# Polysketch attention and an ELU block: pairs of query groups, and the first w_out products earlier

## The chip, the cores and the metric

The kernel runs on one core of one Trainium2 chip. The metric is the time of one execution in device microseconds (us); the median of three runs is given. A separate profiled execution shows where the time lies; its span (first to last instruction) is a few microseconds shorter than the time.

The engines by the names of the profile: PE is TensorE (matrix products; PEld is its loading of weights), DVE is VectorE, ACT is ScalarE, POOL is GpSimd, SP issues transfers.

## The reference

Attention by a sketched polynomial kernel, without a mask, and then a two-layer block with ELU:

```python
q, k, v: (4, 4, 1088, 32)      # batch, heads, sequence, head_dim
S1, S2:  (8, 32)
w_in:    (128, 2048)           # w_out: (2048, 128)

def phi(x):                                    # 64 features per token and head
    a = einsum('rd,bhsd->bhsr', S1, x)
    b = einsum('rd,bhsd->bhsr', S2, x)
    return einsum('bhsi,bhsj->bhsij', a, b).reshape(..., 64)

q_p, k_p = phi(q), phi(k)
kv  = einsum('bhsf,bhsd->bhfd', k_p, v)
z   = sum(k_p, axis=2)
num = einsum('bhsf,bhfd->bhsd', q_p, kv)
den = einsum('bhsf,bhf->bhs', q_p, z)[..., None] + 1e-6
x   = num / den                                # to (4352 tokens, 128)
h   = x @ w_in
g   = where(h > 0, h, exp(min(h, 0)) - 1)
out = g @ w_out
```

The inputs come as 8-byte floats. The kernel reads them as pairs of 32-bit words; for the weights it builds a rounded 4-byte float on the chip in five steps (`round_a` to `round_e`, of which `round_b` is on ScalarE and the others on VectorE).

## The kernel before

The 4352 tokens are 68 half tiles of 64 tokens. Eight half tiles make a query group of 512 tokens; there are nine groups, the last with 256. w_in and w_out are cut into eight blocks `cp` (two times 128 columns or rows each). A step is one block of one group: two products with w_in (`mm1`, tile `h`), ELU on ScalarE and VectorE (`elu_a`, `elu_d`, tiles `e` and `gg`), two products with w_out (`mm2`, tile `o`), which follow two steps later. Groups 0 and 1 share their way through the blocks, since the blocks are still being rounded; later groups run one after the other:

```python
steps = [(0, 0), (0, 1), (1, 0), (1, 1)] + [(g, cp) for cp in range(2, NP) for g in range(2)]
steps += [(g, cp) for g in range(2, NQ) for cp in range(NP)]
```

The attention of the groups from 2 on is put between the steps. A query site holds the products of two groups: `q5` multiplies the features of a group by kv (two halves f), `q1` projects the q of the next group:

```python
def queries(g5, g1, n):
    hs[steps[n]] = [psum.tile([P, 512], F32, name="h", tag="h", bufs=4) for c in range(2)]
    ps = hs[steps[n]] + [psum.tile([P, 512], F32, name="qps", tag="aux") for _ in range(2)]
    if g5 is not None: q5(g5, ps, 0)
    if g1 is not None: q1(g1, ps, g5 is None)
    if g5 is not None: q5(g5, ps, 1)

def q1(g, ps, start=True):
    for c in range(4):                       # a quarter of the group's tokens
        for h in range(H):
            r = slice(D * h, D * h + D)
            for b, t, k, m in parts(g, c):   # two parts where a quarter crosses a batch boundary
                nc.tensor.matmul(ps[h][32 * c:32 * c + 32, P + 64 * k:P + 64 * (k + m)],
                                 SWq[r, b]..., qT[b][r, t:t + m, :]..., tile_position=(D * h, 32 * c))
...
    at(13, queries, None, 2, 14)
    mid(13, q1_out, 2)
    for g in range(2, NQ):
        n = NP * (g - 1)
        n2, n4, n5 = (13, 14, 15) if g == 2 else (n + 3, n + 4, n + 6)
        late(n2, q2, g)                      # denominator and outer product, VectorE
        (mid if g == 2 else late)(n4, q4, g) # transpose of the features, VectorE
        at(n5, queries, g, None if last else g + 1, n5 + 1)
        mid(n5, q5_out, g)                   # x of the group, ScalarE
        if not last: mid(n5, q1_out, g + 1)  # transposes, VectorE
```

`at(n, ...)`, `mid(n, ...)` and `late(n, ...)` put an operation behind the `mm1` of step n, between its two ELU halves, or behind them. `RA(i)`, `RB(i)` are the first two rounding steps of item i of the list `order`, `RC(i)` the last three (four VectorE operations):

```python
order = [(0, 1, 0), (1, 1, 0), (0, 0, 1), (1, 0, 1), (2, 1, 0), (2, 0, 1)] + [(cp, 1, 1) for cp in range(3, NP)]
# (block, w_in?, w_out?)
```

The opening computes the keys of batch 0, the x of groups 0 and 1 and their first products one after another. Its end:

```python
    q5_early(0)              # x of group 0: products xps, copies xg
    q1_second()              # q of group 1, into a tile of the pool "aux"
    mm1_first()              # group 0, block 0
    ...
    RC(1)
    elu_a(0, 0, 0); elu_a(0, 0, 1)
    mm1(0, 1)
    q2(1, 2)                 # group 1: denominator and outer product (qp)
    q4_early(1)              # transposes on TensorE (qtp), copies (qpT)
    for c in range(2): elu_d(0, 0, c)
    round_w(round_c, 2)
    RA(3); RB(3)
    round_w(round_d, 2)
    q5_early(1)              # x of group 1
    keep_warm(1)             # one product that nobody needs (idle)
    round_w(round_e, 2)
    round_w(round_c, 3)
    for c in range(2):
        elu_a(0, 1, c); elu_d(0, 1, c)
        round_w(round_e if c else round_d, 3)
    KC(0)
```

After it the loop begins at step 2 with `mm1(1, 0)` and then `mm2(0, 0)`.

Of the kernel before, what the change touches and what calls it, by code (L numbers as in the profile page):

```python
# [27 lines left out]
def kernel(  # L28
# [8 lines left out]
    moe_w_out: bass.AP,  # L37
    out: bass.AP,
):

# [6 lines left out]
    nc = tc.nc  # L49
# [276 lines left out]
        feats[b, half] = kp  # L326


    def KO_first(t0, t1):
        if t0 == 0:  # L330
            feats[0, 0] = work.tile([P, 5, H, R, R], F32, name="kp", tag="kp", bufs=3)
        a_ = kf_ps[0][:, 64 * t0:64 * t1].rearrange("p (m x r) -> p m x r", x=2, r=R)[:, :, 1, :]
        b_ = feats[0][:, 0, t0:t1].rearrange("p t h r -> p (t h) r")
        m = (t1 - t0) * H
        nc.vector.tensor_mul(feats[0, 0][:, t0:t1].rearrange("p t h i j -> p (t h) i j"),
                             _ap(a_, list(a_.ap[1:]) + [[0, R]]), _ap(b_, [[R, m], [0, R], [1, R]]))

    def KO_pool():
        kp = feats[0, 1] = work.tile([P, 5, H, R, R], F32, name="kp", tag="kp", bufs=3)
        ab = feats[0][:, :, 5:].rearrange("p x t h r -> p (t h) x r")  # L340
        outer(kp[:, :KT - 5].rearrange("p t h i j -> p (t h) i j"), ab, nc.gpsimd)

# [72 lines left out]
    NH = B * NT  # L417
    NQ = (NH + 7) // 8
    qn = [min(8, NH - 8 * g) // 2 for g in range(NQ)]
    abw, ans, qp, qpT, xg = {}, {}, {}, {}, {}  # L420
    pws = [const.tile([P, H * 4, R + 1], F32, name=f"pw{i}") for i in range(2)]
    for pw in pws:
        nc.gpsimd.memset(pw[:, :, R:], 1e-6)

# [32 lines left out]
        return p[:, :128].rearrange("p (t h r) -> p h t r", t=4, h=H)  # L457

    def q1_second():
        p = psum.tile([P, 512], F32, name="abwp", tag="aux")  # L460
        for i in range(4):
            for u in range(2):
                b, t = half_tile(1, 2 * i + u)
                nc.tensor.matmul(p[64 * u:64 * u + 64, i * 96:i * 96 + 96], qT[b][:, t, :],  # L464
                                 SW[:].rearrange("p h x r -> p (h x r)"), skip_group_check=True,
                                 tile_position=(0, 64 * u))
        abw[1] = work.tile([P, H * 4, 3 * R], F32, name="abw1", tag="abq1", bufs=1)
        nc.scalar.copy(abw[1][:].rearrange("p (h t) y -> p h t y", h=H),
                       p[:, :384].rearrange("p (t h y) -> p h t y", t=4, h=H))

    def parts(g, c):

        n = qn[g] // 2
        k = 0
        while k < n:
            b, t = half_tile(g, n * c + k)
            m = min(n - k, NT - t)
            yield b, t, k, m
            k += m
# [3 lines left out]
    def q1(g, ps, start=True):  # L483
        for c in range(4):
            for h in range(H):
                r = slice(D * h, D * h + D)
                for b, t, k, m in parts(g, c):
                    nc.tensor.matmul(ps[h][32 * c:32 * c + 32, P + 64 * k:P + 64 * (k + m)],  # L488
                                     SWq[r, b].rearrange("p x r -> p (x r)"),
                                     qT[b][r, t:t + m, :].rearrange("p t s -> p (t s)"), start=start, stop=True,  # L490
                                     skip_group_check=True, tile_position=(D * h, 32 * c))
        abw[g] = ps

    def q1_out(g):
        ps, n = abw[g], qn[g]
        abw[g] = work.tile([P, H * 4, 4 * R], F32, name="abw", tag="abw", bufs=2)
        for h in range(H):
            nc.vector.transpose(abw[g][:, n * h:n * h + n, :].rearrange("p m y -> p (m y)"), ps[h][:, P:P + 32 * n])  # L498

    def q2(g, parts=1):  # L500
        q2_den(g)
        q2_out(g, parts)

    def q2_den(g, zq=None):
        m = H * qn[g]
        x = abw[g][:, :m, :]
        pw = pws[g % 2]
        if zq is None:
            nc.vector.tensor_mul(pw[:, :m, :R], x[:, :, R:2 * R], x[:, :, 2 * R:3 * R])
        else:  # L510
            nc.vector.tensor_mul(pw[:, :m, :R].rearrange("p (h t) r -> p h t r", h=H),
                                 x[:, :, R:2 * R].rearrange("p (h t) r -> p h t r", h=H), zq)
        den = work.tile([P, 4 * H], F32, name="den", tag="den")
        nc.vector.tensor_reduce(den[:, :m], pw[:, :m], axis=AX, op=ADD)
        nc.vector.reciprocal(den[:, :m], den[:, :m])
        an = work.tile([P, 4 * H, R], F32, name="an", tag="an")
        nc.vector.tensor_mul(an[:, :m], x[:, :, R:2 * R], _ap(den[:, :m], [[1, m], [0, R]]))
        ans[g] = an

# [23 lines left out]
    def q5_early(g):  # L543
        xp = [psum.tile([P, 512], F32, name="xps", tag="aux") for _ in range(2)]
        for h in range(H):
            for w in range(2):
                nc.tensor.matmul(xp[w][D * h:D * h + D, :256], kvS[64 * w:64 * w + 64, h, :],  # L547
                                 qpT[g][64 * w:64 * w + 64, h].rearrange("p m s -> p (m s)"),
                                 skip_group_check=True, tile_position=(64 * w, D * h))
        xg[g] = work.tile([P, 512], F32, name="xg", tag="xg", bufs=2)  # L550
        to = xg[g][:].rearrange("p (m w s) -> p w m s", w=2, s=P)
        for w, copy in enumerate((nc.scalar.copy, nc.vector.tensor_copy if g else nc.scalar.copy)):
            copy(to[:, w], xp[w][:, :256].rearrange("p (m s) -> p m s", s=P))

    def q4(g):

        m = H * qn[g]
        qpT[g] = work.tile([P, 4 * H, 2, 32], F32, name="qpT", tag="qpT", bufs=2)
        nc.vector.transpose(qpT[g][:, :m].rearrange("p m f s -> p (m f s)"),  # L559
                            qp[g][:, :m].rearrange("p m i j -> p (m i j)"))  # L560

    def q5(g, ps, f):
        n = qn[g]
        for h in range(H):
            for c in range(4):
                r = slice(32 * c, 32 * c + 32)
                for j, (b, t, k, m) in enumerate(parts(g, c)):
                    nc.tensor.matmul(ps[c][D * h:D * h + D, 64 * k:64 * (k + m)], kvq[r, b, f, h, :],  # L568
                                     qpT[g][r, n * h + 2 * k:n * h + 2 * (k + m), f, :],
                                     start=(f == 0 and j == 0), stop=(f == 1),  # L570
                                     skip_group_check=True, tile_position=(32 * c, D * h))
        xg[g] = ps

    def q5_out(g):
        ps, n = xg[g], 32 * qn[g]
        xg[g] = work.tile([P, 512], F32, name="xg", tag="xg", bufs=2)
        for c in range(4):

            o = n * c if g < NQ - 1 else n * (2 * (c % 2) + c // 2)
            nc.scalar.copy(xg[g][:, o:o + n], ps[c][:, :n])  # L580

    def queries(g5, g1, n):

# [94 lines left out]
    KF(0)  # L678
    transp(qT, "q", 0, 0, 8)
    q1_first()  # L680
    KO_first(0, 5)
    KO_pool()
    Z_first()
    zq = q1z_first()
    RA(0)
# [19 lines left out]
    mm1(0, 1)  # L705
    q2(1, 2)
    q4_early(1)
    for c in range(2):
        elu_d(0, 0, c)
    round_w(round_c, 2)  # L710
    RA(3)
    RB(3)
    round_w(round_d, 2)
    q5_early(1)
    keep_warm(1)
    round_w(round_e, 2)
    round_w(round_c, 3)
    for c in range(2):
        elu_a(0, 1, c)
        elu_d(0, 1, c)  # L720
        round_w(round_e if c else round_d, 3)
    KC(0)

# [12 lines left out]
    def late(n, f, *a):  # L738
        extra.setdefault((n, 1), []).append((f, *a))

    for n, i in ((2, 3), (3, 4), (4, 6), (5, 5), (6, 7), (8, 8), (10, 9), (12, 10)):
        if i > 3:
            at(n - 1, RA, i)
            late(n - 1, RB, i)
        if i > 3:
            at(n, RC, i, i == 7)

    late(2, make_Sxp)
    late(2, make_SWq)
    late(3, Z_share, 0)  # L750
    late(8, KV_first)
    zls = {}

# [12 lines left out]


    for b, (n_t, n_f, n_o, n_a, n_z) in enumerate(
            ((4, 6, (7, 9), 11, 12), (15, 16, (17, 18), 19, 20), (18, 19, (24, 27), 30, 32)), 1):
        at(n_t, transp, kT, "k", b, 0, NT)  # L770
        at(n_f, KF_late, b)
        late(n_f, KF_late_out, b)
# [3 lines left out]
        late(n_a, sums_out, b)  # L776
        at(n_z, turn, b)
        late(n_z, turned, b)
    late(7, transp, qT, "q", 1, 0, NT)
    at(21, transp, qT, "q", 2, 0, NT)  # L780
    at(30, transp, qT, "q", 3, 0, NT)
    at(13, queries, None, 2, 14)
    mid(13, q1_out, 2)
    for g in range(2, NQ):
        n = NP * (g - 1)
        n2, n4, n5 = (13, 14, 15) if g == 2 else (n + 3, n + 4, n + 6)
        late(n2, q2, g)
        (mid if g == 2 else late)(n4, q4, g)
        last = g + 1 == NQ
        at(n5, queries, g, None if last else g + 1, n5 + 1)  # L790
        mid(n5, q5_out, g)
        if not last:
            mid(n5, q1_out, g + 1)

    N = len(steps)
    for n in range(2, N + 2):
# [12 lines left out]
        g, cp = steps[n - 2]  # L809
        if g == NQ - 1:  # L810
            mm2_last(cp, cp == 0, cp == NP - 1)
        else:
            mm2(g, cp, cp == 0, cp == NP - 1)
            if cp == NP - 1:
                fin1(g)
# [30 lines left out]
```

## Time and profile before

| | |
|---|---|
| time, median of 3 | 281.13 us (281.09 to 281.94) |
| span of the profiled execution | 277.7 us |
| granted TensorE clock | 1.000 |
| PE busy | 271.4 us |
| DVE busy | 180.0 us |
| ACT busy | 181.5 us |
| bytes moved by DMA | 13.42 MB |

How to read the lines. In the chain of waits in order of time the columns are start, duration, engine, tile, line of the kernel, and the number of records; a product of 4-byte floats leaves two records, so `x4` is two products. In the timeline the columns are start, duration, engine, line, operation, output and inputs, shapes, number of records, and in brackets the idle time before it and who ended it. L602 is `mm1`, L639 `mm2`, L568 `q5`, L488 `q1`, L547 and L553 `q5_early`, L541 `q4_early`, L626 `elu_d`, L528 the outer product of the queries, L111 to L124 rounding steps, L216 `keep_warm`.

### The profile page before, as it was taken

Reading aid. Unit: us, or ns where it says so; the run is one execution under the profiler, and the core shown is the slowest. Engines: PE = TensorE matmul, PEld = TensorE weight load, DVE = VectorE, ACT = ScalarE, POOL = GpSimd, SP = SyncE. Lnnn points to the kernel's source line nnn. Section 1 sums busy time; section 2 is a strip of 40 time slices with the busy share of each in tenths; the row PEclk is TensorE's granted clock in tenths of the full one; section 3 lists DMA queues with packets and bytes.
Section 4 is the critical chain, followed back from the end, with each engine's and each line's share of the span. In section 5 each row is a group of like instructions: output and inputs, shape, how many; then the busy total and the mean of one; then the engine's idle time right before and its main releaser. Section 6 shows DMA issues by size and latency. Waiting matters only on the chain.

```text
span 277.7 us, 4925 instructions
## 1 busy us (share of the span) xinstructions
PE 271.4 (98%) x1909; PEld 136.6 (49%) x1909; DVE 180.0 (65%) x336; ACT 181.5 (65%) x352; POOL 14.6 (5%) x39
## 2 busy tenths in 40 slices
PE   8899999999999999999999999999999999999994
PEld 6754434454544544444644454445444444444694
DVE  6998999986968775568344844465346644463442
ACT  2479877774656556666566666665666666667682
POOL 4400009000000000000000000000000000000000
PEclk9999999999999999999999999999999999999999
DMA  6996961100004000011001000020002000100020
GB/s 191 320 336 183 285 179 31 53 0 2 2 0 65 15 0 2 0 26 16 2 0 29 10 2 2 5 34 2 0 0 38 1 2 0 27 11 2 5 35 19
DMA packets 25638, 13.42 MB, mean 48 GB/s; under 512 B 18448, under 2 KB 23824, under 8 KB 25616
## 3 DMA queue, kind: packets, MB, share of 16 engines
q1 hardware_dynamic: 25024, 12.66, 18.1%
q10 hardware_dynamic: 592, 0.46, 0.5%
q8 instruction: 15, 0.25, 0.4%
q14 instruction: 7, 0.06, 0.1%
HBM read 10.88 MB, written 2.23 MB: 47 GB/s over the span
## 4 chain that ended last, share of the span: by engine, by line
PE 97%; ACT 1%; issue 0%; DVE 0%
PE h L602 42%; PE o L639 40%; PE ol L662 3%; PE idle L216 2%; PE kv L358 2%; PE h L568 1%; PE qps L568 1%; PE h L488 1%; PE kfps L307 1%; PE h L609 1%; PE xps L547 1%; PE qps L488 1%; PE qtp L540 1%; PE abp L288 1%; ACT qpT L541 0%; PE abwp L464 0%
## 5 line engine op out<-in xcount | busy, mean ns | idle before, releaser
L626 DVE SCALAR_TENSOR_TENSOR gg<-e,h 128x512 f32<-128x512 f32 (+1 forms) x144 | 93.2, 655 | 83.0 <-ACT e L620 82.8
L602 PE MATMUL h<-xg,W 128*128 128x512 f32 (+1 forms) x284 | 126.8, 569 | 0.1
L618 ACT ACTIVATE e<-h 128x512 f32<-128x512 f32 (+1 forms) x144 | 81.7, 567 | 65.2 <-PE h L602 64.5
L639 PE MATMUL o<-gg,W 128*128 128x512 f32 x256 | 121.5, 597 | 0.0
L620 ACT ACTIVATE e<-e 128x512 f32<-128x512 f32 (+1 forms) x144 | 87.3, 606 | 4.6
L602 PEld LDWEIGHTS h<-xg,W 128*128 128x128 f32 x284 | 53.4, 190 | 61.9 <-issue 49.7
L639 PEld LDWEIGHTS o<-gg,W 128*128 128x128 f32 x256 | 47.3, 190 | 55.6 <-issue 54.3
L103 ACT ACTIVATE W<-W,ebias 128x256 uint32<-128x256 uint32 (+1 forms) x11 | 6.6, 602 | 5.2 <-DVE W L98 5.2
L528 DVE TENSOR_TENSOR qp<-an,abw 128x1024 f32<-128x1024 f32 (+1 forms) x9 | 9.3, 1047 | 0.3
L568 PE MATMUL h<-qpT,kvq 32*32 32x128 f32 (+1 forms) x256 | 8.7, 257 | 0.0
L568 PE MATMUL qps<-qpT,kvq 32*32 32x128 f32 (+1 forms) x224 | 8.7, 271 | 0.0
L662 PEld LDWEIGHTS ol<-W,gg 128*128 128x128 f32 x64 | 8.1, 192 | 0.3
L559 DVE STREAM_TRANSPOSE qpT<-qp 128x1024 f32<-128x1024 f32 (+1 forms) x7 | 8.1, 1161 | 0.0
L662 PE MATMUL ol<-W,gg 128*128 128x128 f32 x64 | 8.1, 275 | 0.0
L580 ACT COPY xg<-h 128x128 f32<-128x128 f32 (+1 forms) x14 | 2.9, 261 | 7.8 <-PE qps L568 5.5
L568 PEld LDWEIGHTS h<-qpT,kvq 32*32 32x32 f32 x256 | 5.4, 103 | 4.7 <-issue 3.8
L111 DVE SCALAR_TENSOR_TENSOR W<-raw,W 128x256 uint32<-128x256 uint32 (+1 forms) x11 | 7.6, 694 | 0.0
L216 PE MATMUL idle<-some 128*128 128x256 f32 (+2 forms) x16 | 5.8, 493 | 1.2 <-DVE warm L142 1.2
L498 DVE STREAM_TRANSPOSE abw<-h 128x128 f32<-128x128 f32 (+1 forms) x14 | 3.5, 288 | 4.8 <-ACT xg L580 4.8
L272 POOL TENSOR_TENSOR kp<-abk 128x1024 f32<-128x1024 f32 (+1 forms) x3 | 6.5, 2167 | 1.6 <-ACT abk L296 1.6
L116 DVE SCALAR_TENSOR_TENSOR raw<-raw 128x256 f32<-128x256 uint32 (+1 forms) x11 | 6.1, 554 | 0.3
L358 PEld LDWEIGHTS kv<-kp,v 128*32 128x32 f32 x288 | 4.8, 110 | 2.3 <-issue 1.5
(115 smaller groups left out, 148.5 us busy)
## 6 DMA issues: line engine op xcount, KB each, us to landing
raw<-in_moe_w_in_dram SPq DMA_DIRECT2D x8, 256.0 KB, 6.1
raw<-in_moe_w_out_dram SPq DMA_DIRECT2D x8, 256.0 KB, 6.4
hd_k<-in_k_dram SPq DMA_DIRECT2D x3, 544.0 KB, 7.7
hd_q<-in_q_dram SPq DMA_DIRECT2D x3, 544.0 KB, 3.5
out_dram<-ob SPq DMA_DIRECT2D x40, 32.0 KB, 1.7
v<-in_v_dram SPq DMA_DIRECT2D x4, 288.0 KB, 6.5
v<-in_v_dram SPq DMA_DIRECT2D x4, 256.0 KB, 7.6
hd_k<-in_k_dram SPq DMA_DIRECT2D x1, 288.0 KB, 3.8
```

The source lines that it names most:

```text
L111: nc.vector.scalar_tensor_tensor(d, hi, 0x80000000, d, op0=AND, op1=OR)
L216: nc.tensor.matmul(idle[:, :cols], some[:, :P], some[:, :cols], skip_group_check=True)
L358: nc.tensor.matmul(kv[32 * h:32 * h + 32, :R * R], vt[b][:, (h * KT + i) * D:(h * KT + i + 1) * D], kp[i // 5][:, i % 5, h].rearrange("p i ...
L528: nc.vector.tensor_mul(qp[g][:, h], _ap(a_, list(a_.ap[1:]) + [[0, R]]), _ap(b_, [b_.ap[1], [0, R], b_.ap[2]]))
L559: nc.vector.transpose(qpT[g][:, :m].rearrange("p m f s -> p (m f s)"), qp[g][:, :m].rearrange("p m i j -> p (m i j)"))
L568: nc.tensor.matmul(ps[c][D * h:D * h + D, 64 * k:64 * (k + m)], kvq[r, b, f, h, :], qpT[g][r, n * h + 2 * k:n * h + 2 * (k + m), f, :], st ...
L602: nc.tensor.matmul(hs[g, cp][c][:, :n], W[:, cp, c * P:c * P + P], xg[g][:, :n])
L618: nc.scalar.activation(e, hs[g, cp][c][:, :n], RELU, scale=-1.0)
L620: nc.scalar.activation(e, e, EXP, scale=-1.0)
L626: nc.vector.scalar_tensor_tensor(gs[g, cp][:, c, :n], es[g, cp][:, c, :n], -1.0, hs[g, cp][c][:, :n], op0=ADD, op1=MAX)
L639: nc.tensor.matmul(ops[g][:, :n], W[:, cp, (2 + c) * P:(3 + c) * P], gg[:, c, :n], start=(first and c == 0), stop=(last and c == 1))
L662: nc.tensor.matmul(ops[g][i][:], gg[:, c, i * P:i * P + P], W[:, cp, (2 + c) * P:(3 + c) * P], start=(first and c == 0), stop=(last and c ...
```

## The change

Four things. First, groups 4 and 5, and 6 and 7, are handled as a pair (`units`): one query site instead of two, with products, transposes and copies twice as wide; features of a pair are made in two halves of two heads each. Second, `mm2(0, 0)` goes between the x of group 1 and its first products, in place of `keep_warm`, and the rounding steps around it are ordered by when their block is needed. Third, the first outer product of the keys is shared differently between VectorE and GpSimd, so that GpSimd can start after the first of ScalarE's two copies. Fourth, smaller moves: the products of `q1_second` go to a tile of the pool `h`, both copies of group 1's x go to ScalarE, and the transposes of q and some work of batch 3 move to other steps. The aim is to take small products and idle time off TensorE.

```diff
+    def KO_pool():                                   # GpSimd: tiles 0 to 3 of the first half
+        ...
+        ab = feats[0][:, :, :4].rearrange("p x t h r -> p (t h) x r")
+        outer(feats[0, 0][:, :4].rearrange("p t h i j -> p (t h) i j"), ab, nc.gpsimd)
...
-    KO_first(0, 5)
     KO_pool()
+    KO_first(4, 5)
+    KO_first(5, KT)
@@ q1_second
-        p = psum.tile([P, 512], F32, name="abwp", tag="aux")
+        p = psum.tile([P, 512], F32, name="abwp", tag="h", bufs=4)
@@ q5_early
-        for w, copy in enumerate((nc.scalar.copy, nc.vector.tensor_copy if g else nc.scalar.copy)):
-            copy(to[:, w], xp[w][:, :256].rearrange("p (m s) -> p m s", s=P))
+        for w in range(2):
+            nc.scalar.copy(to[:, w], xp[w][:, :256].rearrange("p (m s) -> p m s", s=P))
@@ queries
+    units = {g: ([g, g + 1] if 4 <= g < NQ - 1 else [g]) for g in [2, 3] + list(range(4, NQ, 2))}
+    un = {g: sum(qn[x] for x in gr) for g, gr in units.items()}
     def parts(g, c):
-        n = qn[g] // 2
+        n = un[g] // 2
 ... (q1, q1_out, q2_den, q4, q5, q5_out take un[g] for qn[g]; q1 writes from column 256 on)
+    def q2_half(g, i):                               # outer product of two of the four heads
+        ...
+    def q5_out(g, i=0):                              # x of the first or second group of a pair
+        ...
@@ end of the opening
     q2(1, 2)
     q4_early(1)
-    for c in range(2):
-        elu_d(0, 0, c)
-    round_w(round_c, 2)
     RA(3)
+    elu_d(0, 0, 0)
+    RC(2)
     RB(3)
-    round_w(round_d, 2)
+    elu_d(0, 0, 1)
     q5_early(1)
-    keep_warm(1)
-    round_w(round_e, 2)
-    round_w(round_c, 3)
+    mm2(0, 0, True, False)
+    RC(3)
     for c in range(2):
         elu_a(0, 1, c)
+    RA(4)
+    RB(4)
+    for c in range(2):
         elu_d(0, 1, c)
-        round_w(round_e if c else round_d, 3)
-    KC(0)
@@ between the steps
-            ((4, 6, (7, 9), 11, 12), (15, 16, (17, 18), 19, 20), (18, 19, (24, 27), 30, 32)), 1):
+            ((4, 6, (7, 9), 11, 12), (15, 16, (17, 18), 19, 20), (18, 19, (24, 25), 27, 28)), 1):
-    late(7, transp, qT, "q", 1, 0, NT)
+    late(10, transp, qT, "q", 1, 0, NT)
     at(21, transp, qT, "q", 2, 0, NT)
-    at(30, transp, qT, "q", 3, 0, NT)
+    late(24, transp, qT, "q", 3, 0, NT)
+    for n, g, nx in ((13, None, 2), (15, 2, 3), (22, 3, 4), (30, 4, 6), (46, 6, 8), (62, 8, None)):
+        at(n, queries, g, nx, n + 1)
+        if g is not None:
+            mid(n, q5_out, g)
+        if nx is not None:
+            mid(n, q1_out, nx)
+        if g is not None and len(units[g]) > 1:
+            late(n, q5_out, g, 1)
 ... (q2_den, q2_half and q4 of each unit at steps of their own)
@@ the loop
-        else:
+        elif n > 2:
             mm2(g, cp, cp == 0, cp == NP - 1)
```

In the batch rows, the last two numbers are the steps of the key products with v (`KA`) and of the turn of kv and z; for batch 3 they move from 30 and 32 to 27 and 28. `KC(0)` moves behind step 3. Item 4 of the rounding (w_in of block 2) moves ahead of step 2.

More of the change, by code (lines that the diff above doesn't have):

```diff
@@ L326, in KO @@
         feats[b, half] = kp
+    def KO_pool():
+        for half in range(2):
+            feats[0, half] = work.tile([P, 5, H, R, R], F32, name="kp", tag="kp", bufs=3)
+        ab = feats[0][:, :, :4].rearrange("p x t h r -> p (t h) x r")
+        outer(feats[0, 0][:, :4].rearrange("p t h i j -> p (t h) i j"), ab, nc.gpsimd)
     def KO_first(t0, t1):
-        if t0 == 0:
-            feats[0, 0] = work.tile([P, 5, H, R, R], F32, name="kp", tag="kp", bufs=3)
-        a_ = kf_ps[0][:, 64 * t0:64 * t1].rearrange("p (m x r) -> p m x r", x=2, r=R)[:, :, 1, :]
+        half, o = divmod(t0, 5)
+        n = t1 - t0
+        a_ = kf_ps[half][:, 64 * o:64 * (o + n)].rearrange("p (m x r) -> p m x r", x=2, r=R)[:, :, 1, :]
         b_ = feats[0][:, 0, t0:t1].rearrange("p t h r -> p (t h) r")
[L334 to L341, printed above, removed]
+        nc.vector.tensor_mul(feats[0, half][:, o:o + n].rearrange("p t h i j -> p (t h) i j"),
+                             _ap(a_, list(a_.ap[1:]) + [[0, R]]), _ap(b_, [[R, n * H], [0, R], [1, R]]))
     def z_tile(b, ps, i):
@@ L419 @@
     qn = [min(8, NH - 8 * g) // 2 for g in range(NQ)]
-    abw, ans, qp, qpT, xg = {}, {}, {}, {}, {}
-    pws = [const.tile([P, H * 4, R + 1], F32, name=f"pw{i}") for i in range(2)]
+    abw, ans, qp, qpT, xg, xps = {}, {}, {}, {}, {}, {}
+    pws = [const.tile([P, H * 8, R + 1], F32, name=f"pw{i}") for i in range(2)]
     for pw in pws:
@@ L487, in q1 @@
                 for b, t, k, m in parts(g, c):
-                    nc.tensor.matmul(ps[h][32 * c:32 * c + 32, P + 64 * k:P + 64 * (k + m)],
+                    nc.tensor.matmul(ps[h][32 * c:32 * c + 32, 256 + 64 * k:256 + 64 * (k + m)],
                                      SWq[r, b].rearrange("p x r -> p (x r)"),
@@ L494, in q1_out @@
     def q1_out(g):
-        ps, n = abw[g], qn[g]
-        abw[g] = work.tile([P, H * 4, 4 * R], F32, name="abw", tag="abw", bufs=2)
+        ps, n = abw[g], un[g]
+        pair = n > 4
+        abw[g] = work.tile([P, H * n if pair else H * 4, 4 * R], F32, name="abw", tag="abwp" if pair else "abw",
+                           bufs=1 if pair else 2)
         for h in range(H):
-            nc.vector.transpose(abw[g][:, n * h:n * h + n, :].rearrange("p m y -> p (m y)"), ps[h][:, P:P + 32 * n])
+            nc.vector.transpose(abw[g][:, n * h:n * h + n, :].rearrange("p m y -> p (m y)"),
+                                ps[h][:, 256:256 + 32 * n])
     def q2(g, parts=1):
@@ L504, in q2_den @@
     def q2_den(g, zq=None):
-        m = H * qn[g]
+        m = H * (un[g] if g > 1 else qn[g])
         x = abw[g][:, :m, :]
@@ L512, in q2_den @@
                                  x[:, :, R:2 * R].rearrange("p (h t) r -> p h t r", h=H), zq)
-        den = work.tile([P, 4 * H], F32, name="den", tag="den")
+        den = work.tile([P, 8 * H], F32, name="den", tag="den")
         nc.vector.tensor_reduce(den[:, :m], pw[:, :m], axis=AX, op=ADD)
         nc.vector.reciprocal(den[:, :m], den[:, :m])
-        an = work.tile([P, 4 * H, R], F32, name="an", tag="an")
+        an = work.tile([P, 8 * H, R], F32, name="an", tag="an")
         nc.vector.tensor_mul(an[:, :m], x[:, :, R:2 * R], _ap(den[:, :m], [[1, m], [0, R]]))
@@ L549, in q5_early, with heads, q4 @@
                                  skip_group_check=True, tile_position=(64 * w, D * h))
-        xg[g] = work.tile([P, 512], F32, name="xg", tag="xg", bufs=2)
+        xg[g] = work.tile([P, 512], F32, name="xg", tag="xg", bufs=3)
         to = xg[g][:].rearrange("p (m w s) -> p w m s", w=2, s=P)
-        for w, copy in enumerate((nc.scalar.copy, nc.vector.tensor_copy if g else nc.scalar.copy)):
[L553 to L560, printed above, removed]
+        for w in range(2):
+            nc.scalar.copy(to[:, w], xp[w][:, :256].rearrange("p (m s) -> p m s", s=P))
+    def heads(g):
+        return 2 if un[g] > 4 else H
+    def q2_half(g, i):
+        m = heads(g) * un[g]
+        r = slice(m * i, m * i + m)
+        qp[g, i] = work.tile([P, 4 * H, R, R], F32, name="qp", tag="qp", bufs=2)
+        a_, b_ = ans[g][:, r], abw[g][:, r, :R]
+        nc.vector.tensor_mul(qp[g, i][:, :m], _ap(a_, list(a_.ap[1:]) + [[0, R]]),
+                             _ap(b_, [b_.ap[1], [0, R], b_.ap[2]]))
+    def q4(g, i=0):
+        m = heads(g) * un[g]
+        qpT[g, i] = work.tile([P, 4 * H, 2, 32], F32, name="qpT", tag="qpT", bufs=2)
+        nc.vector.transpose(qpT[g, i][:, :m].rearrange("p m f s -> p (m f s)"),
+                            qp.pop((g, i))[:, :m].rearrange("p m i j -> p (m i j)"))
     def q5(g, ps, f):
-        n = qn[g]
+        n = un[g]
         for h in range(H):
+            i, o = divmod(h, heads(g))
             for c in range(4):
@@ L568, in q5 @@
                     nc.tensor.matmul(ps[c][D * h:D * h + D, 64 * k:64 * (k + m)], kvq[r, b, f, h, :],
-                                     qpT[g][r, n * h + 2 * k:n * h + 2 * (k + m), f, :],
+                                     qpT[g, i][r, n * o + 2 * k:n * o + 2 * (k + m), f, :],
                                      start=(f == 0 and j == 0), stop=(f == 1),
                                      skip_group_check=True, tile_position=(32 * c, D * h))
[L572 to L577, printed above, removed]
+        xps[g] = ps
+    def q5_out(g, i=0):
+        ps, n, gr = xps[g], 32 * un[g], units[g]
+        x = xg[g + i] = work.tile([P, 512], F32, name="xg", tag="xg", bufs=3)
+        cs = range(4 // len(gr))
+        for c in cs:
             o = n * c if g < NQ - 1 else n * (2 * (c % 2) + c // 2)
-            nc.scalar.copy(xg[g][:, o:o + n], ps[c][:, :n])
+            nc.scalar.copy(x[:, o:o + n], ps[c + len(cs) * i][:, :n])
     def queries(g5, g1, n):
@@ L739, in late @@
         extra.setdefault((n, 1), []).append((f, *a))
[L741 to L746, printed above, removed]
+    at(2, RC, 4)
+    for n, i in ((4, 6), (5, 5), (6, 7), (8, 8), (10, 9), (12, 10)):
+        at(n - 1, RA, i)
+        late(n - 1, RB, i)
+        at(n, RC, i, i == 7)
     late(2, make_Sxp)
@@ L750 @@
     late(3, Z_share, 0)
+    late(3, KC, 0)
     late(8, KV_first)
@@ L778 @@
         late(n_z, turned, b)
-    late(7, transp, qT, "q", 1, 0, NT)
+    late(10, transp, qT, "q", 1, 0, NT)
     at(21, transp, qT, "q", 2, 0, NT)
-    at(30, transp, qT, "q", 3, 0, NT)
[L782 to L793, printed above, removed]
+    late(24, transp, qT, "q", 3, 0, NT)
[7 more added lines that the diff above has]
+            late(n, q5_out, g, 1)
+    late(13, q2_den, 2)
+    late(13, q2_half, 2, 0)
+    mid(14, q4, 2)
+    late(19, q2_den, 3)
+    late(19, q2_half, 3, 0)
+    late(20, q4, 3)
+    late(22, q2_den, 4)
+    at(26, q2_half, 4, 0)
+    late(26, q2_half, 4, 1)
+    late(27, q4, 4, 0)
+    late(28, q4, 4, 1)
+    late(31, q2_den, 6)
+    late(32, q2_half, 6, 0)
+    late(36, q2_half, 6, 1)
+    late(37, q4, 6, 0)
+    late(38, q4, 6, 1)
+    late(59, q2_den, 8)
+    late(59, q2_half, 8, 0)
+    late(60, q4, 8)
     N = len(steps)
```

## The prediction

> **What bounds the kernel now.** I read the page's engine shares first, then the chain of waits, then the chain in order of time at three places, then VectorE's timeline.
>
> ```profile
> PE 271.4 (98%) x1909; PEld 136.6 (49%) x1909; DVE 180.0 (65%) x336; ACT 181.5 (65%) x352; POOL 14.6 (5%) x39
> PE 97%; ACT 1%; issue 0%; DVE 0%
> ```
>
> The reader is to see that the chain that ends last lies on TensorE for 97% of the span: nothing else is on it for long, so only two things can shorten this kernel: less TensorE time, or a TensorE gap in the opening closed. The chain's pieces say what a steady step costs. A step is one pair of 128-column blocks for one group of 512 tokens: two products with w_in (`h`), two with w_out (`o`). In order of time, around the queries of group 4 (step 22) and at the end (step 62):
>
> ```profile
> 101.36 1.72 PE h L602 x4
> 103.07 0.23 PE h L568 x2
> ...
> 104.49 1.91 PE o L639 x4
> 106.40 0.86 PE h L602 x2
> ```
> ```profile
> 248.88 1.72 PE h L602 x4
> 250.59 0.17 PE h L568 x2
> ...
> 251.38 1.91 PE o L639 x4
> ```
>
> A pair of products is 1.72, a step 3.43. 64 full steps give 219.7, and the eight half-size steps of the last group, at 0.86 + 0.89, another 14.0: 233.7 of 277.7 is work the change leaves alone. The rest is the opening, the end, and small products wedged between the steps. Such a place costs its own length plus 0.19: the first large pair behind it takes 1.91, not 1.72. Step 22 is 104.49 - 103.07 = 1.42 + 0.19; step 62 is 0.79 + 0.19.
>
> The opening, in the same view, just before the steady steps:
>
> ```profile
> 20.53 0.60 ACT qpT L541
> 21.12 0.04 issue
> 21.17 1.15 PE xps L547 x16
> 22.32 0.63 PE idle L216 x2
> 22.94 0.06 issue
> 23.00 1.96 PE h L602 x4
> 24.96 1.72 PE o L639 x4
> ```
>
> `idle` is a product nobody needs; it fills the wait for ScalarE and VectorE to copy group 1's x. VectorE's timeline for the same stretch, without the lines that don't matter:
>
> ```profile
> 18.43 1.29 DVE L528 TENSOR_TENSOR qp<-an,abw 128x512 f32<-128x512 f32 x2
> 19.64 1.43 DVE L626 SCALAR_TENSOR_TENSOR gg<-e,h 128x512 f32<-128x512 f32 x2
> 20.99 0.42 DVE L111 SCALAR_TENSOR_TENSOR W<-raw,W 128x256 uint32<-128x256 uint32 x1
> ...
> 22.43 0.42 DVE L553 COPY xg<-xps 128x256 f32<-128x256 f32 x1 [0.16 <-PE xps L547]
> 22.78 0.42 DVE L124 SCALAR_TENSOR_TENSOR W<-raw,W 128x256 f32<-128x256 f32 x1
> ```
>
> Operations follow one another without a hole: here VectorE is the engine that decides when the first w_out block is rounded (23.20, the end of the last line).
>
> [...] Here PE is 98% busy while weight loading is 49%, so I count from the chain's steps and not from the share. [...] the same 128x256 masking that takes 0.25 to 0.29 elsewhere takes 0.85 from 9.44 to 10.29, beside GpSimd's outer product, which ends at 10.14.
>
> **The change, part by part.**
>
> *1. Query groups 4 and 5, and 6 and 7, go through as pairs.* Their small products are 256 columns wide instead of 128, and there are query sites at steps 13, 15, 22, 30, 46, 62 instead of 13, 15, 22, 30, 38, 46, 54, 62. A site is made of phases of 16 products in 32x32 tiles (fp32 makes each two records): one q1 phase, two q5 phases. Step 22 has three phases at 128 columns in 1.42, so 0.473 each; step 62 has two at 64 columns in 0.79, so 0.395. The slope is 0.08 to 0.10 per 64 columns (step 54, 128/64/128 columns, 1.31, gives 0.36 for its 64-column phase). A 256-column phase is then 0.473 + 2 x 0.1 = about 0.67, against 2 x 0.473 for the two it replaces. Where a quarter of the tokens crosses a batch boundary, four more products come in: step 38 has one such phase in three and takes 1.63, step 46 has two and takes 1.65. I put 0.12 to 0.2 on each.
>
> Before, steps 22 to 62: 1.42 + 1.42 + 1.63 + 1.65 + 1.31 + 0.78 = 8.21.
> After: step 22 (two phases at 128, one at 256 with a boundary) 1.77; step 30 (three at 256, boundaries in all) 3 x 0.67 + 3 x 0.12 = 2.37; step 46 (two at 256 with boundaries, one at 64) 1.34 + 0.24 + 0.38 = 1.96; step 62 0.78. Sum 6.88.
> Saved: 1.33. Two sites less save two returns at 0.19, but the third batch's key products, which before shared the return of step 30 (132.15 to 134.91 without a large pair between), move to step 27 and pay their own: net 0.19. Together 1.5, all of it TensorE time on the chain.
>
> *2. Group 0's first w_out products take the place of `idle`.* The 1.72 of `o` at 24.96 moves to the hole. It needs the first w_out block and both halves of `gg`. VectorE now does, from 19.69: masking of block 3 (0.2), `gg` half one (0.65), four rounding steps of the w_out block (1.67 in the row of the first block, 13.71 to 15.38), `gg` half two (0.65). So the block is ready near 22.3, half two near 22.9. Group 1's `xps` end near 21.8, since part 3 gives TensorE half a microsecond. `o` runs from 22.3 with 0.2 for the switch to about 24.25, when x of group 1 is long copied. Then `h`, `h`, `o` of group 1 and block 1 follow: 24.25 + 3 x 1.72 = 29.4. Before, the same four pairs were through at 30.11. Gain 0.7. It is less than 1.72, since `o` can't start before VectorE has rounded its weights.
>
> *3. q1 of group 1 takes a buffer of the other pool.* Before, its products waited at 15.53 for ScalarE's copy of group 0's x; now they run before it, and `h` can start near 15.8 instead of 16.41. But VectorE's chain to `qp` (19.72 at the end) doesn't wait on them, so by itself this gains nothing at the end; it only makes `xps` early for part 2.
>
> *4. The first outer product is split anew between VectorE and GpSimd.* VectorE does 256 + 1024 elements in two operations (0.40 + 1.22 estimated from the rows 1.49 for 1280 and 1.20 for 1024) instead of one of 1.49; the second waits for ScalarE's second copy at 8.10 and ends near 9.37, so z's mask (9.33 before) is some 0.05 late. GpSimd starts 0.45 earlier and stops disturbing the masking at 9.44. But what follows, `pw` at 10.29, waits for TensorE's zqp, which ends at 10.24. Net: 0 to -0.05.
>
> *5. The same rounding in another order, VectorE's x copy moved to ScalarE, the transpose of batch 1's q moved from step 7 to step 10.* No TensorE work; it only shifts slack. I count 0.
>
> Sum: 1.5 + 0.7 = 2.2 of 281.13: **278.9**.
>
> **The rivals.**
>
> *VectorE becomes the bound in the weight stage.* VectorE runs from 28.28 to 62 without holes. In the stretch where blocks are rounded, `gg` of step 4 ends at 36.60 and the products of step 6 that reuse its buffer start at 37.14; at step 10 `gg` of step 8 ends at 52.17 and the second product starts near 52.8. Slack is 0.5 to 0.6, and TensorE arrives 0.7 earlier. For a stall: GpSimd's two outer products block a rounding operation for 2.38 at 46.66. Against: 0.42 of copying and 0.65 of holes leave VectorE's list before step 4, and the 1.30 transpose leaves it before step 8. If VectorE wins, the 0.7 goes and the time is 279.6.
>
> *The wide query phases scale with their columns.* If a phase at 256 columns cost twice one at 128, only 0.2 would be saved by part 1, and the time is 280.2. Against it stands the measured fixed part: halving the columns at step 62 took away only a sixth.
>
> *A new wait behind the pair sites.* VectorE's four transposes are now 256 wide (about 0.43 instead of 0.29) and wait for ScalarE's copies; `h` of the next step needs two of these buffers. Copies end about 0.75 and transposes about 1.35 behind the site, and the large pair in between lasts 1.91. So it should fit, with 0.5 left. If not, each of two sites loses some tenths: 279.5.
>
> *More than I count.* If `o` closes the hole wholly and the boundaries cost nothing at 256 columns, 0.3 and 0.7 more are gained: 277.9.
>
> **Range and chances.** The three runs of before spread over 0.85, part 1 is uncertain by 0.6, part 2 by 0.5, mostly towards less. I take 277.6 to 280.3. For 2% the time would have to pass 275.5 or 286.8; the TensorE work counted leaves no room for the first, and no wait in the list is long enough for the second: faster 0.02, same 0.97, slower 0.01.
>
> **What would show it.** In the changed profile: `o` before `h` of group 1, starting at 22.3 +/- 0.3 behind the rounding of the w_out block on VectorE; the product of step 4 near 29.4. Sites at steps 22, 30, 46 of 1.8, 2.4, 2.0 in the chain. A steady step of 3.43 everywhere else, TensorE still 97% of the chain, and a span near 275.5. I am wrong if a product of steps 6 to 12 waits on `gg`, if a 256-column phase takes over 0.8, or if a product behind a pair site waits on a transpose.

## The result, and the profile after

| | before | after |
|---|---|---|
| time, median | 281.31 us | 279.84 us |
| ratio (95% interval) | | 0.9947 (0.9925 to 0.9968) |
| PE, DVE, ACT busy | 271.4, 180.0, 181.5 us | 272.5, 177.7, 180.9 us |

1.47 us less: within the range, two thirds of the 2.2 that I worked out. Two repeats beside other kernels gave 0.9933 and 0.9925.

First a trap. The span of this profile is 278.5, longer than the 277.7 of before, though the times are shorter. The timeline of TensorE in the opening says why; before the change first, then after:

```profile
5.40 0.70 PE L216 MATMUL idle<-some 128*128 128x256 f32 x2
6.03 1.67 PE L288 MATMUL abp<-Sab,kT 128*64 128x64 f32 x36
```
```profile
5.57 1.22 PE L217 MATMUL idle<-some 128*128 128x256 f32 x2
6.72 2.56 PE L289 MATMUL abp<-Sab,kT 128*64 128x64 f32 x33
```

The same products take nearly twice as long, and VectorE's masking of z starts 2.35 later (11.68 against 9.33). Nothing in front of them was changed. A second profile of the changed kernel (the last repeat) has them at 0.70 and 1.67 again, and a span of 276.0. And a kernel with the opening of before (the single queries below) has them long, with a span of 279.4:

```profile
6.72 2.56 PE L288 MATMUL abp<-Sab,kT 128*64 128x64 f32 x33
```

So the long products don't belong to the change. The trace's list of granted clocks differs along with them: it has its first entry, full clock, at 5.17 us before and at 10.75 in this profile. The views count the time ahead of the first entry as full clock and show 1.00 there. That the clock makes the products long isn't shown. The profile of before, of an execution of 279.61, and this one, of 280.35, differ by more than the change. I compare openings with the second profile, 1.7 below before, and everything behind the opening with either.

In the second profile, the end of the opening in the chain in order of time:

```profile
21.50 0.44 DVE W L125
21.94 0.04 issue
21.98 1.98 PE o L662 x4
23.97 3.43 PE h L625 x8
27.40 1.72 PE o L662 x4
29.12 1.72 PE h L625 x4
```

The reader is to see that `o` stands where `idle` stood, that it is released by L125, the last rounding step of its own weights on VectorE, and that the pair of step 4 starts at 29.12, not 30.11. VectorE's timeline before it, in the order that the change gave:

```profile
18.23 1.29 DVE L536 TENSOR_TENSOR qp<-an,abw 128x512 f32<-128x512 f32 x2
19.44 0.29 DVE L99 TENSOR_SCALAR W<-raw 128x256 uint32<-128x256 uint32 x1
19.65 0.68 DVE L649 SCALAR_TENSOR_TENSOR gg<-e,h 128x512 f32<-128x512 f32 x1
20.25 0.42 DVE L112 SCALAR_TENSOR_TENSOR W<-raw,W 128x256 uint32<-128x256 uint32 x1
...
21.50 0.43 DVE L125 SCALAR_TENSOR_TENSOR W<-raw,W 128x256 f32<-128x256 f32 x1
21.85 0.68 DVE L649 SCALAR_TENSOR_TENSOR gg<-e,h 128x512 f32<-128x512 f32 x1
```

Then the pair site at step 46, in the chain of the first profile after (before, this site stood at 192.26 and took 1.65, and another stood at step 54 and took 1.31):

```profile
192.05 1.72 PE h L625 x4
193.77 0.85 PE h L589 x15
...
196.31 1.91 PE o L662 x4
```

196.31 - 193.77 = 2.54; I had said 1.96. At step 30 after, and at step 46 before, the first large pair takes more than the usual 1.91:

```profile
136.03 0.84 PE h L589 x17
...
138.57 1.98 PE o L662 x4
```
```profile
192.26 0.17 PE h L568
...
193.91 1.96 PE o L639 x4
```

What is over 1.91 belongs to the site: 2.54 + 0.07 = 2.61 after, and 1.65 + 0.05 = 1.70 before. The same reading for all query sites:

| step | before | said | after |
|---|---|---|---|
| 13, 15 | 0.78, 1.68 | the same | 0.78, 1.68 |
| 22 | 1.41 | 1.77 | 1.91 |
| 30 (without the key products of before) | 1.42 | 2.37 | 2.61 |
| 38 | 1.63 | none | none |
| 46 | 1.70 | 1.96 | 2.54 |
| 54 | 1.31 | none | none |
| 62 | 0.78 | 0.78 | 0.78 |
| sum from 22 on | 8.25 | 6.88 | 7.84 |

So the pairs save 0.4 and not 1.33 at the sites. Where it goes is visible inside the site; TensorE's timeline of the first profile after, from the first product of step 46 on (a line takes neighbouring records together and shows the form of the first):

```profile
193.70 0.41 PE L589 MATMUL h<-qpT,kvq 32*32 32x192 f32 x2
193.72 0.40 PE L589 MATMUL qps<-qpT,kvq 32*32 32x256 f32 x2
193.73 0.41 PE L589 MATMUL h<-qpT,kvq 32*32 32x192 f32 x2
193.75 0.41 PE L589 MATMUL qps<-qpT,kvq 32*32 32x256 f32 x2
193.76 0.41 PE L589 MATMUL h<-qpT,kvq 32*32 32x192 f32 x2
193.78 0.41 PE L589 MATMUL qps<-qpT,kvq 32*32 32x256 f32 x2
193.80 0.53 PE L589 MATMUL h<-qpT,kvq 32*32 32x192 f32 x5
...
194.02 0.38 PE L589 MATMUL qps<-qpT,kvq 32*32 32x256 f32 x2
194.05 0.61 PE L589 MATMUL h<-qpT,kvq 32*32 32x64 f32 x9
194.35 0.41 PE L589 MATMUL qps<-qpT,kvq 32*32 32x256 f32 x2
```

A phase goes head by head, and a head has four tiles, one for each quarter. The quarter with the batch boundary comes first: its first part of 192 columns, then its second part of 64 columns in the same tile, then the other three quarters, one into `h` and two into `qps`. The second parts start only from 194.05 on, each 0.35 behind the first part in its tile; that they wait for the tile is my reading, no view names what they wait for. Yet the other quarters of the first three heads, which stand behind them, have started by 193.80; all that shows of a second part at its place is a step of 0.013 instead of 0.007 between the starts around it. The stop comes behind the first part of the fourth head (193.80): the `qps` products of that head start at 194.35, 0.55 later. (The `qps` line of 194.02 is second records of earlier products.) At step 13 the products behind the stop are in tiles without a second part. There the split quarter, four tiles with 64 and 64 columns, stands at the head of the phase:

```profile
67.25 0.25 PE L493 MATMUL h<-qT,SWq 32*32 32x64 f32 x2
67.28 0.25 PE L493 MATMUL qps<-qT,SWq 32*32 32x64 f32 x2
67.31 0.30 PE L493 MATMUL h<-qT,SWq 32*32 32x128 f32 x2
...
67.35 0.30 PE L493 MATMUL qps<-qT,SWq 32*32 32x128 f32 x4
67.39 0.23 PE L493 MATMUL h<-qT,SWq 32*32 32x64 f32 x2
...
67.52 0.38 PE L493 MATMUL h<-qT,SWq 32*32 32x128 f32 x3
67.69 0.31 PE L493 MATMUL qps<-qT,SWq 32*32 32x128 f32 x2
```

The second parts start from 67.39 on, but the eight products of the next two quarters stand behind them and have started by 67.35. The late ones, from 67.52 and 67.69 on, are the four of the last quarter, which have their tiles to themselves. Counted in the kernel's order, with the second parts, it is the same at both steps: of the first 8 + 4 + 4 products at step 13 and 5 + 5 + 5 + 1 at step 46, sixteen each time, all but the second parts have started within 0.10, and the seventeenth and those behind it start later. A phase without a boundary has just sixteen. With a boundary it has twenty, and here three or four of the late ones are full products, which start 0.2 to 0.6 behind the sixteenth.

### The profile page after: what moved, and what is told of

Read it like the earlier page. It is cut to its first block, busy times and chain, and to the rows that moved or that the text cites. A ratio compares the mean times of both kernels' runs of the same rounds, so it can differ in the third digit from the quotient of the medians.

```text
span 278.5 us, 4558 instructions
## 1 busy us (share of the span) xinstructions
PE 272.5 (98%) x1739; PEld 138.1 (50%) x1739; DVE 177.7 (64%) x320; ACT 180.9 (65%) x345; POOL 15.0 (5%) x39
## 4 chain that ended last, share of the span: by engine, by line
PE 93%; DVE 4%; POOL 1%; issue 1%; ACT 0%; DVEq 0%
PE h L625 41%; PE o L662 40%; PE ol L685 3%; PE h L589 2%; PE idle L217 2%; PE kv L359 1%; DVE qp L536 1%; PE abp L289 1%; POOL kp L273 1%; PE kfps L308 1%; PE qps L589 1%; PE qps L493 1%; PE h L493 1%; DVE raw L117 0%; DVE W L125 0%
## 5 line engine op out<-in xcount | busy, mean ns | idle before, releaser
L589 PE MATMUL qps<-qpT,kvq 32*32 32x128 f32 (+2 forms) x160 | 8.8, 311 | 0.0
L589 PE MATMUL h<-qpT,kvq 32*32 32x64 f32 (+3 forms) x208 | 8.3, 275 | 0.0
L572 DVE TENSOR_TENSOR qp<-an,abw 128x1024 f32<-128x1024 f32 (+1 forms) x7 | 8.0, 1141 | 0.1
L112 DVE SCALAR_TENSOR_TENSOR W<-raw,W 128x256 uint32<-128x256 uint32 (+1 forms) x11 | 6.9, 631 | 0.0
L603 ACT COPY xg<-h 128x128 f32<-128x128 f32 (+2 forms) x10 | 2.5, 300 | 6.7 <-PE qps L589 3.8
L505 DVE STREAM_TRANSPOSE abw<-h 128x128 f32<-128x128 f32 (+2 forms) x10 | 3.1, 339 | 4.8 <-ACT xg L603 4.8
```

Of the source, the lines that this page charges most:

```text
L572: nc.vector.tensor_mul(qp[g, i][:, :m], _ap(a_, list(a_.ap[1:]) + [[0, R]]), _ap(b_, [b_.ap[1], [0, R], b_.ap[2]]))
```

## The experiments

The theory at the start: both parts of the change work, the opening with 0.7 or a little more, the pairs with 0.6, and what is missing is lost at the batch boundaries, where a second product follows in a tile that is still busy. Rivals: VectorE takes the opening's lead back; wide phases simply scale with their columns; the extra products cost by their number.

**The opening alone.** The kernel before with the new opening; the queries stay single, with sites at 13, 15, 22, 30, 38, 46, 54, 62. From its edit:

```diff
-    KO_first(0, 5)
     KO_pool()
+    KO_first(4, 5)
+    KO_first(5, KT)
...
-    keep_warm(1)
+    mm2(0, 0, True, False)
...
-    late(7, transp, qT, "q", 1, 0, NT)
+    late(10, transp, qT, "q", 1, 0, NT)
```

> The new opening alone (early w_out products, order of rounding, split of the outer product, q1 buffer, copies on ScalarE); query sites as before. My theory: the opening gives 0.7 us, so the ratio to before is 0.9975 and half of the whole effect is here. Rival: the opening gives nothing that lasts, because VectorE takes the lead back in the weight stage; ratio 1.000 and a wait of a step 6 to 12 product on gg.

Measured: 0.9961 (0.9938 to 0.9983), about 1.1 us. From the end of `qp` to the pair of step 4 it takes 29.17 - 19.59 = 9.58, before 30.11 - 19.72 = 10.39: 0.8. A further 0.16 comes from that pair itself, which took 1.88 before and 1.72 now, and 0.13 from an earlier end of `qp`; together 1.1. Its chain:

```profile
22.03 1.98 PE o L639 x4
24.02 3.43 PE h L602 x8
27.45 1.72 PE o L639 x4
29.17 1.72 PE h L602 x4
```

From here to step 13 the large pairs follow one another at 1.72, with only the known small products between them. No product of steps 6 to 12 waits for `gg`: the rival falls.

**The pairs alone.** The changed kernel with the opening of before (`KO_first(0, 5)` first, q1 of group 1 in `aux`, `keep_warm(1)`, VectorE's copy, the old order of rounding).

> The pairs alone, with the opening of before. My theory after the changed profile: sites of 1.9, 2.5, 2.5 and 0.8 at steps 22, 30, 46, 62 instead of 8.2 in all, and one return less, so 0.6 to 0.8 us less: ratio 0.9973. Rival: the pairs give all of the 1.5 us: ratio 0.9948.

Measured: 0.9984 (0.9959 to 1.0008), 0.45 us; sites 1.92, 2.61, 2.54, 0.78. The time alone doesn't exclude zero, but the sites agree with the profile after to 0.01, and the interval shuts out the 1.5 of the rival. The span is 277.1, 0.6 under before. The times of each kernel fall into two groups about 2 us apart (before: 279.4 to 280.5 and 281.2 to 282.1), and by the medians of the groups the pairs save 0.8 and 0.6. The two parts alone give 1.1 + 0.45 = 1.55, the whole change 1.47: they add up.

**No boundaries.** What is left out: a quarter that crosses a batch boundary is treated as if it lay in one batch, so for those tokens the wrong kv is used; only the time is of interest.

```diff
             b, t = half_tile(g, n * c + k)
-            m = min(n - k, NT - t)
-            yield b, t, k, m
-            k += m
+            yield b, min(t, NT - n), k, n
+            k += n
```

> The changed kernel with every quarter of a group treated as lying in one batch: the extra small products at batch boundaries are left out, and with them the right operands for these tokens. My theory: the boundaries are what made the wide sites longer than I worked out (2.5 instead of 2.0 at step 46); without them the sites at steps 22, 30, 46 take 1.62, 2.0 and 1.73, and the kernel takes about 1.5 us less than the changed one: 278.3. Rival: a wide phase simply scales with its columns; then step 30 stays above 2.4 and under 0.4 us are gained.

Measured: 277.63, ratio 0.9871 (0.9835 to 0.9907). Site 46 in its chain:

```profile
189.88 1.72 PE h L624 x4
191.60 0.34 PE h L588 x2
...
193.34 1.91 PE o L661 x4
```

1.74, and steps 22, 30: 1.62, 2.06. I had said 1.62, 2.0 and 1.73. The sizes of the phases (0.473 at 128 columns, 0.67 at 256) were right; the rival of scaling falls. The boundaries cost 0.29, 0.55 and 0.80 at these three sites, and 0.35 and 0.27 at steps 13 and 15 (0.43 and 1.41 here).

**The second part at the end of its phase.** Complete; only the order of products changes.

```diff
+    def rest_last(g, tiles):
+        todo = [(j, c, h, *x) for c, h in tiles for j, x in enumerate(parts(g, c))]
+        return [(c, h, j, *x) for j, c, h, *x in sorted(todo, key=lambda y: y[0])]
 def q5(g, ps, f):
-        for h in range(H):
-            for c in range(4):
-                for j, (b, t, k, m) in enumerate(parts(g, c)):
+        for c, h, j, b, t, k, m in rest_last(g, [(c, h) for h in range(H) for c in range(4)]):
 # q1 in the same way
```

> The changed kernel, complete, but where a quarter crosses a batch boundary the product for its second part comes at the end of its phase and not directly behind the first part in the same 32x32 tile. Theory A: the second part waits for the first in its tile and holds up the products behind it; moved to the end it overlaps with the other tiles and the kernel gains 0.5 to 1.0 us on the changed one (279.0). Theory B: the cost is that of four more products and their weight loads wherever they stand; then under 0.2 us are gained.

Measured: 278.40, ratio to before 0.9899 (0.9865 to 0.9934). Its repeat:

> The complete kernel with the second parts at the end once more, on the same chip as the others of this call, for its interval: ratio to before 0.990, sites 1.70, 2.39, 1.90, 0.79 again.

278.35, 0.9882 (0.9843 to 0.9921), beside the changed kernel once more:

> The changed kernel beside the one with the second parts at the end, on the same chip: ratio to before 0.994, 0.4 to 0.5% above the other; sites 1.91, 2.54, 2.54, 0.78 again.

279.69, 0.9925 (0.9898 to 0.9952). So the new order takes a further 1.34 off on the same chip. Site 46 of the first of these, in the chain:

```profile
189.26 1.72 PE h L625 x4
...
191.40 0.41 PE h L589 x9
...
192.88 1.91 PE o L662 x4
```

The large pair of 189.26 ends at 190.98: the site is 1.90. The sites at 13, 15, 22, 30, 46 are 0.58, 1.59, 1.70, 2.40, 1.90, in all 1.36 less than after. The number of products is the same, so most of the boundaries' cost of 2.26 came from their order: theory B falls, and the gain is larger than theory A said. But the wait isn't the one that theory A names. The sixteen that start together are now the first parts, within 0.10 again (190.90 to 191.00), and those behind, from 191.28 on, are the four narrow second parts instead of three wide products and one narrow. What stays against no boundaries (0.15, 0.18, 0.07, 0.34, 0.16) may be the extra products themselves; that wasn't taken apart.

**The second part three products later.** The same sort, but within each row of four tiles.

```diff
-        todo = [... for c, h in tiles ...]
+        for i in range(0, len(tiles), 4): sort tiles[i:i + 4] alone
```

> Like the kernel with the second parts at the end of the phase, but they come after the other three first parts of the same row of four tiles, so three products behind their first part instead of up to fifteen. Theory A (the tile is busy for as long as the product before it lasts, some 0.3 us, and the second part waits for that, with everything behind it): three products, issued within 0.05 to 0.1 us, are too short a distance; site 46 stays above 2.2 us (2.54 directly behind, 1.90 at the end). Rival (only standing directly behind the first part costs[...]): site 46 falls to 1.9 to 2.0.

Measured: 0.9925 (0.9902 to 0.9947), sites 1.84, 2.59, 2.52. In the chain at step 46:

```profile
192.24 1.72 PE h L628 x4
193.96 0.62 PE h L592 x12
...
196.48 1.91 PE o L665 x4
```

Three products between them change almost nothing, as theory A said, so the rival of the neighbourhood falls. The trace gives another reason than theory A, though. Again the last of the first 5 + 5 + 5 + 1 products starts at 193.99, and the wide ones of the fourth head start late (the two in `qps` at 194.43 and 194.54), though no second part of their own head stands in front of them. Both orders leave the same wide products behind the sixteenth, and both sites take the same time (2.52 and 2.54). That the number sixteen decides it is my reading of these traces; no run varied it, so a limit isn't shown.

**Single queries with the second part last.** The kernel before with `rest_last` in q1 and q5, nothing else.

> The kernel before, with nothing but the second parts at the end of their phase; sites stay 128 columns wide. If a second part costs because its tile is still busy, it costs less where the first part is short: boundaries at 128 columns cost 0.2 to 0.35 us per site, and moving the parts should win back about half, 0.5 to 0.6 us over the five sites with a boundary (13, 15, 38, 46 of before): ratio 0.998. Rival: the gain is the same 1.3 us as in the wide sites; ratio 0.995.

Measured: 0.9979 (0.9955 to 1.0004). Sites 13, 15, 38, 46: 0.58, 1.58, 1.53, 1.59 instead of 0.78, 1.68, 1.63, 1.70, in all 0.5 less. That is 0.08 for each of six split phases, where the wide ones (six phases at steps 22, 30, 46) gained 0.18: where the products that come late are only 128 columns wide, less is won by putting narrow ones in their place. Doubled width and order thus belong together: 0.45 and 0.6 us alone, 1.9 of the 3.0 that the best version gains (its 3.0 less the opening's 1.1).

**Block 3 later in the opening.** On top of the second part at the end.

```diff
-    RA(3)
     elu_d(0, 0, 0)
     RC(2)
-    RB(3)
+    RA(3)
     elu_d(0, 0, 1)
     q5_early(1)
+    RB(3)
```

> The kernel with the second parts at the end, and in the opening the masking of block 3 behind the rounding of the first w_out block, its ScalarE step behind the copies of group 1's x. VectorE's chain decides when the first w_out products start, so they start 0.2 us earlier and the kernel gains 0.2 us, if the later rounding of block 3 doesn't hold up the ELU of group 0, block 1. Rival: TensorE waits for something else there; nothing moves.

Measured: 278.78, 0.9925 (0.9892 to 0.9958); too wide to show 0.2. In the profile, `o` follows the start of `qp` by 23.55 - 20.02 = 3.53 instead of 22.51 - 18.75 = 3.76, and TensorE's hole before `o` is 0.19 instead of 0.42:

```profile
23.06 0.43 DVE L125 SCALAR_TENSOR_TENSOR W<-raw,W 128x256 f32<-128x256 f32 x1
23.41 0.29 DVE L99 TENSOR_SCALAR W<-raw 128x256 uint32<-128x256 uint32 x1
23.43 0.65 ACT L563 COPY xg<-xps 128x256 f32<-128x256 f32 x2 [0.79 <-PE xps L557]
23.55 1.98 PE L662 MATMUL o<-gg,W 128*128 128x512 f32 x4 [0.19 <-DVE W L125]
```

VectorE's chain does decide the start of `o`; in time this is inconclusive.

**A filler in the opening, and the changed kernel again.** `keep_warm(1)` once more between the two small products, on top of the second part at the end.

> The kernel with the second parts at the end, with one more 256-column filler product between the two small products of the opening (near 4.6 us). In half of the executions seen so far the products from 5.6 to 9.4 us take twice their time, and the whole time is about 2 us longer. [...] the filler makes it rarer and the median falls towards 276.9; the price is up to 0.4 us later keys. If it is a matter of the moment of start alone, the median stays at 278.4 or rises to 278.8.

Measured: 279.34, 0.9921 (0.989 to 0.9953), no better than without it (0.9899 and 0.9882), and its profile has the long products again (1.22 and 2.56). The filler doesn't help. The repeat of the changed kernel:

> The changed kernel once more, beside the others on the same chip: 0.9947 of the time before, and a second look at its opening. If the twice as long small products of its first profile belong to the change, they are there again; if they come and go with the execution, they may be absent, and the first w_out products then start near 22.1 to 22.3 us instead of 24.57.

0.9933 (0.9912 to 0.9954). Here the idle pair takes 0.70 and the key products 1.75, but q's transfer comes late instead, and VectorE waits 1.02 for it:

```profile
7.61 0.71 DVE L231 STREAM_TRANSPOSE qT<-hd_q 128x512 f32<-128x512 f32 x1 [1.02 <-DMA hd_q<-in_q_dram]
```

The mean granted clock of this execution is 0.992 (1.000 in the second profile), and `o` starts at 23.65. So the opening varies in more than one way. The late transfer was seen only in profiles with the new opening (waits of 1.02 here and of 0.33, 1.54 and 1.05 in three of the experiments above); whether it has to do with the change isn't shown.

## Why the prediction was right in size and where it was wrong

- *The opening (part 2), said 0.7 and `o` at 22.3*: right in mechanism, a little low in size. `o` at 21.98, 0.8 in the chain up to step 4; the 0.16 at the pair of step 4 wasn't foreseen; 1.1 (0.5 to 1.7) in time. That it couldn't begin before VectorE had rounded its weights was right too: the hole before it is 0.4, ended by L125.
- *VectorE's chain, the q1 buffer (part 3)*: `qp` still ends 19.5 to 19.7 in the undisturbed openings, and q1 earlier gave nothing there, as said. The buffer alone wasn't tried.
- *The split of the first outer product (part 4), said 0*: in the first profile after the masking takes 0.29 (11.79 to 12.08, when GpSimd's outer product has ended at 11.24) instead of 0.85, and `pw` (the first step of the denominator) waits 0.55 for zqp; from z's mask to `pw` it is 0.96 before and 0.95 after. Right.
- *The pairs (part 1), said 1.5*: the mechanism was right and one term mis-sized. The phase widths held without boundaries: the sites came out 0.01 to 0.05 above the sums. The step that failed is "I put 0.12 to 0.2 on each" for a quarter that crosses a boundary. I took this from sites 128 columns wide and carried it over unchanged. At 256 columns it came to 0.29 for one phase at step 22, 0.55 for three at step 30, 0.80 for two at step 46, in all 1.64 where the sums held 0.75. The 0.89 between is nearly all that the sites miss of the 1.33. Most of it was the order: full products stood behind the sixteenth of their phase and started late, and with the narrow second parts in their place 1.06 of the 1.64 went away.
- *The rivals*: none was it. VectorE held no product of steps 6 to 12 up. The 0.2 that I gave the rival of scaling was wrong by its own terms: with 0.946 for a wide phase and the boundaries that I put in, the sites come to 8.54, and part 1 would have lost 0.1; no boundaries settles it all the same. Behind the pair sites the next `h` starts right after the large pair (196.31 + 1.91 = 198.22), so copies and transposes fit.
- *The range*: it held the time although the pairs gave less than a third of what was said at the sites; that the opening gave more than said, and so made up for part of it, was luck.

At step 46 the starts don't follow the kernel's order: the 64-column second part comes second in it and starts at 194.05 at the earliest, while a `qps` product behind it starts at 193.72. A product that starts late let those right behind it go first, at both steps within the first sixteen of the phase.

## What to carry to other kernels

When small products are packed into tiles of the array, write down their order and see which of them come late: in these traces the first sixteen 32x32 products of a phase started within 0.10 us, but for second parts in a tile already in use, and full products behind the sixteenth started 0.2 to 0.6 us after it. The wider the late ones were, the more the order was worth (0.18 against 0.08 for a phase). Issue one product for every tile first and the narrow remainders after; here that order was worth about as much again as the whole change, and the kernel with both is 1.1% faster than before. And when a cost taken from one size is carried to another, ask first whether it is a fixed cost or a wait for something that grows.

## What the runs showed that I had not expected

- The small products between 5.6 and 9.4 us can take nearly twice their time (256 columns twice: 1.22 instead of 0.70) in one execution and not in the next, of the same code; the whole is then some 2 us longer (spans of 278.5 and 276.0 in the two profiles compared above). Five of the thirteen profiles have them long. Why some executions do stays open, and the filler changed nothing.
- With boundaries left out, a phase of 16 fp32 products in 32x32 tiles took about 0.68 at 256 columns where 0.473 was read at 128 and 0.39 at 64. By these three, an estimate, some 0.3 of a phase doesn't depend on its width, more than half of it at 128 columns.
- Why step 46 loses 0.40 for each split phase and step 30 only 0.18 isn't settled. At 46 the first part is 192 columns wide, at 30 it is 128 in two phases of three; the last of the three has 192 as well.
